# Two SBUF pools trade places and one look-up table moves behind a later product, in a three-stage kernel on one core

## The chip, the cores and the metric

The kernel runs on one core of a Trainium2 chip. The metric is device microseconds of one execution, the median of a few runs. The core has a matrix engine (PE, with its weight loads in a row of their own, PEld), a vector engine (DVE), an engine for activations and copies (ACT), GpSimd (POOL), and a queue engine (SP) that issues most DMAs. Each engine works through its own list of instructions in order, and they wait for each other by semaphores.

## The reference

Three layers, one after the other, in float32:

```python
# attention over 4 x 8 heads, 576 tokens, head size 64
proj = x @ w_phi;  proj -= max(abs(proj));  phi = [exp(proj), exp(-proj)]      # for q and for k
kv = phi(k).T @ v;  z = sum(phi(k));  x = (phi(q) @ kv) / (phi(q) @ z + 1e-6)
# experts: each of 2304 tokens goes to one of 8
logits = x @ w_gate + bias[modality];  e = argmax(logits);  g = softmax(logits)[e]
x[tokens of e] = g * (relu(x[tokens of e] @ w1[e]) @ w2[e])
# last products
out = ((x @ w_a) * (x @ w_b)) @ w_out
```

Float32 products of the last two layers are made of three matmuls each, on a high and a low part of both operands (`mm3`, L53 to L56).

## The kernel before, in words

**Attention** runs in rounds, each on one group of heads (eight groups; rounds 0 to 8, a round also finishes what the round before it began). `phi` (L125) projects raw q and k (`qk`, pool `a_ld`, two buffers of 9216 bytes a partition), subtracts the maximum and leaves the differences `df` (pool `a_df`, five buffers of 4096 bytes). `turn` transposes a `df` on PE (`qtp`) and ACT writes its exponentials (`qts`). `kx` multiplies exponentials of k with v (`kxp`, copied by DVE to `kx`), `num` makes the numerator and denominator (`nmp`), and DVE divides (`rec`, `x`, L237 to L242). Within the rounds PE's order is the order of the code; on the other engines, and everywhere after the rounds, a scheduler that simulates a timeline sets it when the program is built.

**Routing** handles the tokens in two halves; `Route.steps` (L339) lists what is done for one half: gate, rank, place, table. `table` makes two look-up tables by one-hot matmuls: `tbp` gives `idx`, the rows that the experts gather, and `tbq` gives `perm` and `g2`, the way back and the squared gate weight, which only the last stage reads. POOL builds the one-hots of the first half, DVE those of the second. The first half's table stands in round 7, before `phi(1)` (L924); the second half's steps are side work of the expert stage (L952).

**Experts** (`Moe`, L520 to L603) take four tiles of up to 608 tokens, two for each half. A tile gathers its tokens in five pieces (`xg`, L561), transposes them (`mxt`, L573) and splits them into high and low (`mxh` on ACT, `mxl` on DVE). Eight blocks of weights are loaded (`s`, two buffers) and split (`wh` on ACT, `wl` on DVE, three buffers). Eight `hp` products of 24 matmuls each follow, their results split into `hh` (ACT) and `hl` (DVE), and then `yp` products, copied out by ACT. `hp` and `yp` share three PSUM buffers. The pools of this stage lie on the same side of SBUF that `a_ld` and `a_df` held: `m_w` (the `wh` and `wl`, 24 KB) first, `m_xt` (the `mxh` and `mxl`, 19 KB) behind it. A tile of a new pool waits until the last reader of what lay there has finished.

As further side work each half of the last layer's weights is converted: a load `raw` (SP), `cvs` on ACT, `cvs` on POOL, then `cvt`, `cvt`, `cvs`, `cvs`, `wsum` on DVE (L691 to L698), sums, a split `whi` (ACT, one buffer), and a store from which the buffer comes free.

**Last products** (from some 400 us to the end) keep PE busy nearly throughout.

Of the kernel before, what the change touches and what calls it, by code (L numbers as in the profile page):

```python
# [10 lines left out]
F32 = mybir.dt.float32  # L11
F32R = mybir.dt.float32r
BF16 = mybir.dt.bfloat16
I32 = mybir.dt.int32
AF = mybir.ActivationFunctionType
ALU = mybir.AluOpType
# [4 lines left out]
P = 128  # L21
B, H, S, D = 4, 8, 576, 64
NTOK = B * S
HALF = NTOK // 2
# [4 lines left out]
NG = 9  # L29
# [3 lines left out]
NTMAX = (HALF + E * (TS - 1)) // TS  # L33
KMAX = (HALF + TS - 1) // TS
NSUB = (TS + P - 1) // P
YC = HALF + CG
TB = 6
# [21 lines left out]
class Attn:  # L59
    def __init__(self, nc, tc, ctx, cst, qk, v, vt, xs, lgp):  # L60
        self.nc, self.tc = nc, tc
        self.qk, self.v, self.vt, self.xs = qk, v, vt, xs
        self.cst, self.lgp = cst, lgp
        pool = lambda n, b, **kw: ctx.enter_context(tc.tile_pool(name=n, bufs=b, **kw))
        self.p_ld = pool("a_ld", 2, side="right")
        self.p_df = pool("a_df", 5, side="right")
        self.p_v = pool("a_v", 3)
        self.p_x = pool("a_x", 2)
        self.p_sm = pool("a_sm", 4)
        self.p_kx = pool("a_kx", 2)  # L70
        self.p_qt = pool("a_qt", 11)
        self.p_vt = pool("a_vt", 2)
        self.p_kp = pool("a_kp", 4)
        self.p_kt = pool("a_kt", 3)
        self.ps_p = pool("aps_p", 2, space=PSUM)
        self.ps_q = pool("aps_q", 2, space=PSUM)
        self.ps_c = pool("aps_c", 2, space=PSUM)
        self.u = {}
# [185 lines left out]
def consts(nc, pool, keep, w_phi, w_gate):  # L264
    c = {}
    ident = c["ident"] = keep.tile([P, P], F32, name="ident")
    w = c["wp"] = pool.tile([P, P], F32, name="wp")
    nc.scalar.dma_start(out=w[0:64, :], in_=w_phi)
    nc.scalar.dma_start(out=w[64:128, :], in_=w_phi)
    make_identity(nc, ident)  # L270
    mask = c["mask"] = pool.tile([P, 2], F32, name="mask")
    wg = c["wg"] = pool.tile([P, 4, 16], F32, name="wg")
    nc.gpsimd.memset(wg, 0.0)
    src = w_gate.rearrange("(p h d) e -> h d p e", h=2, d=64)
    for h in range(2):
        rows = slice(64 * h, 64 * h + 64)
        nc.gpsimd.memset(mask[rows, h:h + 1], 0.0)
        nc.gpsimd.memset(mask[rows, 1 - h:2 - h], -1000.0)
        nc.gpsimd.dma_start(out=wg[rows, :, 8 * h:8 * h + 8], in_=src[h])
    return c  # L280
# [53 lines left out]
class Route:  # L334
# [4 lines left out]
    def steps(self, wk, ps, tag, after=None):  # L339
        self.wk, self.ps, self.tag = wk, ps, tag  # L340

        def start():
            with self.tc.issue_after(after) if after else nullcontext():
                self.cst = route_consts(self.nc, wk)
            self.gate()

        return [start, self.rank, self.place, self.table]

    def w(self, shape, name, dt=F32):
        return self.wk.tile([P] + shape, dt, tag=name, name=name)  # L350
# [45 lines left out]
    def place(self):  # L396
# [66 lines left out]
        self.meta = self.pool.tile([1, 3 * NTMAX + 1], I32, name=f"meta{self.bp}")  # L463
        nc.vector.tensor_copy(self.meta, meta[0:1, :])

    def table(self):
        nc, c = self.nc, self.cst
        NC = NTMAX * NSUB
        gp = self.w([3, NG], "gp", BF16)
        rest = self.w([NG], "grest")  # L470
        nc.vector.tensor_copy(rest, self.gt)
        for i in range(3):
            nc.vector.tensor_copy(gp[:, i, :], rest)
            if i < 2:
                nc.vector.tensor_sub(rest, rest, gp[:, i, :])

        def onehot(out, i, v, n):
            if not self.bp:
                for g in range(NG):
                    nc.gpsimd.tensor_scalar(out=out[:, g, :], in0=c[i][:, :n], scalar1=v[:, g:g + 1], scalar2=None,  # L480
                                            op0=ALU.is_equal)
                return
            nc.vector.tensor_tensor(out=out, in0=c[i][:, :n].unsqueeze(1).to_broadcast([P, NG, n]),
                                    in1=v.unsqueeze(2).to_broadcast([P, NG, n]), op=ALU.is_equal)

        def lookup(name, col, n, row, parts):
            k = len(parts)
            hot = self.w([NG, n], name + "h", BF16)
            rhs = self.w([NG, k, n], name + "r", BF16)
            lhs = self.w([NG, P], "lhs" if self.bp else name + "l", BF16)  # L490
            onehot(hot, "icol", col, n)
            for i, v in enumerate(parts):
                (nc.vector if self.bp else nc.gpsimd).tensor_mul(rhs[:, :, i, :], hot, v.unsqueeze(2).to_broadcast([P, NG, n]))
            onehot(lhs, "i128", row, P)
            ps = self.ps.tile([P, 512], F32, tag=self.tag, name=name)
            for g in range(NG):
                nc.tensor.matmul(ps[:, :k * n], lhs[:, g, :], rhs[:, g].rearrange("p a n -> p (a n)"),
                                 start=g == 0, stop=g == NG - 1)
            return [ps[:, i * n:(i + 1) * n] for i in range(k)]

        def token(out, hi, lo, base):
            t = self.w([NC], "tk")[:, :hi.shape[1]]
            nc.vector.tensor_scalar(out=t, in0=hi, scalar1=float(1 << TB), scalar2=float(base), op0=ALU.mult, op1=ALU.add)
            nc.vector.tensor_add(out, t, lo)

        toks = [c["tokp"][:, i, :] for i in range(2)]
        self.idx = self.pool.tile([P, NC], I32, name=f"idx{self.bp}")
        self.g2 = self.pool.tile([P, NG], F32, name=f"g2{self.bp}")
        self.perm = self.pool.tile([P, NG], I32, name=f"perm{self.bp}")
        hi, lo = lookup("tbp", self.col, NC, self.pl, toks)  # L510
        token(self.idx, hi, lo, 0)
        hi, lo, *gs = lookup("tbq", self.cq, NG, self.cl, toks + [gp[:, i, :] for i in range(3)])
        token(self.perm, hi, lo, HALF * self.bp)
        nc.vector.tensor_copy(self.g2, gs[2])
        nc.vector.tensor_add(self.g2, self.g2, gs[1])
        nc.vector.tensor_add(self.g2, self.g2, gs[0])
        nc.vector.tensor_mul(self.g2, self.g2, self.g2)
# [362 lines left out]
def low(tc, step):  # L880
    def run():
        with tc.high_priority(offset=-LOWR):
            step()

    return run
# [3 lines left out]
def trn_kernel(ctx, tc, qk, v, vt, w_phi, mod_id, w_gate, bias, wm, wf, out):  # L889
    nc = tc.nc  # L890
# [9 lines left out]
    with ExitStack() as actx:  # L900
        cpool = actx.enter_context(tc.tile_pool(name="const", bufs=1))
        wkpool = actx.enter_context(tc.tile_pool(name="rwork", bufs=1))
        lgp = [(cpool, keep)[i].tile([P, NG, E], F32, name=f"lgp{i}") for i in range(2)]
        with tc.tile_pool(name="warm_ps", bufs=1, space=PSUM) as wps:
            z = cpool.tile([P, 512], BF16, name="warm")
            nc.vector.memset(z, 0.0)
            wz = wps.tile([P, 512], F32, name="warmp")
            for i in range(NWARM):
                nc.tensor.matmul(wz, z[:, :P], z, start=i == 0, stop=i == NWARM - 1)
        cst = consts(nc, cpool, keep, w_phi, w_gate)  # L910
        cst["warm"] = z
        at = Attn(nc, tc, actx, cst, qk, v, vt, xs, lgp)
        at.load(0)
        for r in range(9):
            if r + 1 < 8:
                at.load(r + 1)
            if r == 2:
                bs = bias_load(nc, cpool, keep, bias, mod_id)
                routes = [Route(tc, rpool, lgp[i], bs[i], i) for i in range(2)]
                rsteps = [low(tc, st) for st in routes[0].steps(wkpool, at.ps_c, "c", at.first)]  # L920
            if r == 0:
                order = ExitStack()
                order.enter_context(tc.manual_schedule(engines={mybir.EngineType.PE}))
            at.round(r, {4: {2: rsteps[:1]}, 5: {2: rsteps[1:3]}, 7: {0: rsteps[3:]}}.get(r, {}) if r > 2 else {})  # L924
            if r == 8:
                order.close()
    with ExitStack() as mctx:
# [21 lines left out]

        wk1 = rctx.enter_context(tc.tile_pool(name="rwork1", bufs=1, **tl))  # L950
        rs = routes[1].steps(wk1, ps_t, "t")
        side = {k: [low(tc, rs[f])] for f, k in enumerate((0, 3, 5, 8))}  # L952
        side[9] = [close_work]

        def conv(f):
# [24 lines left out]
        with tc.If(nts[0] > NTMIN, label="extra"):  # L980
            n = slice(3 * NTMAX, 3 * NTMAX + 1)
# [4 lines left out]
    side = {}  # L986
# [65 lines left out]
```

## Time and profile before

| | |
|---|---|
| runs of the kernel before | 828.99 to 831.8 us, median 831.49 us (3 runs) |
| the profiled execution | 832.01 us, its span 830.2 us, mean granted clock 0.996 |
| PE busy | 800.1 us (96%), 7283 matmuls |
| DVE busy | 597.2 us (72%) |
| ACT busy | 375.7 us (45%) |
| POOL busy | 136.3 us (16%) |

The timeline has four stretches of interest here: the last attention rounds (141 to 166 us), the first expert tile with the first conversions (166 to 220), the stretch to the third tile (220 to 260), whose tokens come from the second half, and the rest. In a row of the timeline the first number is the start, the second the length; "[1.88 <-DVE mxl L577]" says that the engine had been idle for 1.88 us and what ended that. The length of a single matmul overlaps the next one, so the step between two matmuls is the difference of their starts.

### The profile page before, as it was taken

Reading aid. Unit: us, or ns where it says so; the run is one execution under the profiler, and the core shown is the slowest. Engines: PE = TensorE matmul, PEld = TensorE weight load, DVE = VectorE, ACT = ScalarE, POOL = GpSimd, SP = SyncE. Lnnn points to the kernel's source line nnn. Section 1 sums busy time; section 2 is a strip of 40 time slices with the busy share of each in tenths; the row PEclk is TensorE's granted clock in tenths of the full one; section 3 lists DMA queues with packets and bytes.
Section 4 is the critical chain, followed back from the end, with each engine's and each line's share of the span. In section 5 each row is a group of like instructions: output and inputs, shape, how many; then the busy total and the mean of one; then the engine's idle time right before and its main releaser. Section 6 shows DMA issues by size and latency. Waiting matters only on the chain.

```text
span 830.2 us, 18334 instructions
## 1 busy us (share of the span) xinstructions
PE 800.1 (96%) x7283; PEld 752.1 (91%) x7284; DVE 597.2 (72%) x1071; ACT 375.7 (45%) x665; POOL 136.3 (16%) x164
## 2 busy tenths in 40 slices
PE   8999999999997999999899999999999999999996
PEld 7989888889997999999799899989999999999995
DVE  6877898779997999996698755675554485445553
ACT  4555555535443564554444433553333354333332
POOL 1000009442225623220121000020000002000002
PEclk9999999999999999999999999999999999999999
DMA  8756432576768887976689866576656668565632
GB/s 301 227 148 177 151 117 82 155 229 218 275 215 288 295 332 246 318 267 229 233 309 324 288 229 212 198 257 209 226 199 199 195 209 291 203 201 184 224 129 87
DMA packets 85163, 184.22 MB, mean 222 GB/s; under 512 B 27760, under 2 KB 37520, under 8 KB 85072
## 3 DMA queue, kind: packets, MB, share of 16 engines
q1 hardware_dynamic: 81872, 173.21, 61.7%
q0 software_dynamic: 3040, 9.72, 3.5%
q8 instruction: 58, 0.95, 0.5%
q14 instruction: 33, 0.27, 0.1%
q10 hardware_dynamic: 160, 0.07, 0.0%
HBM read 145.21 MB, written 37.75 MB: 220 GB/s over the span
## 4 chain that ended last, share of the span: by engine, by line
PE 30%; issue 16%; DVE 2%; ACT 1%; DMA 1%; POOL 0%; POOLq 0%; SPq 0%; DVEq 0%; ACTq 0%
PE abp L54 6%; PE abp L56 6%; PE abp L55 6%; PE op L56 4%; PE op L55 4%; PE op L54 4%; DMA wsc<-whi 1%; POOL out L797 0%; DVE ca L827 0%; ACT pc L841 0%; DVE gl L829 0%; ACT yh L744 0%; DVE d L850 0%; DVE yl L745 0%; DVE ca L855 0%
## 5 line engine op out<-in xcount | busy, mean ns | idle before, releaser
L841 ACT COPY pc<-abp 128x384 f32<-128x384 f32 x252 | 120.4, 479 | 201.7 <-PE abp L56 196.5
L54 PE MATMUL abp<-yh,fw 128*128 128x384 f32 x504 | 169.9, 337 | 2.8 <-ACT pc L841 1.8
L55 PE MATMUL abp<-yl,fw 128*128 128x384 f32 x504 | 169.9, 337 | 0.0
L56 PE MATMUL abp<-yh,fw 128*128 128x384 f32 x504 | 169.9, 337 | 0.0
L54 PEld LDWEIGHTS abp<-yh,fw 128*128 128x128 f32 x504 | 94.6, 188 | 12.1 <-ACT pc L841 3.1
L55 PEld LDWEIGHTS abp<-yl,fw 128*128 128x128 f32 x504 | 94.6, 188 | 7.5
L56 PEld LDWEIGHTS abp<-yh,fw 128*128 128x128 f32 x504 | 94.6, 188 | 0.0
L690 POOL TENSOR_SCALAR cvs<-cvs 128x768 f32<-128x768 f32 x24 | 61.7, 2573 | 196.2 <-ACT cvs L689 147.6
L56 PE MATMUL op<-fw,gl 128*128 128x512 f32 x216 | 85.2, 394 | 1.2 <-DVE gl L829 1.2
L54 PE MATMUL op<-fw,gh 128*128 128x512 f32 x216 | 85.4, 395 | 1.0 <-ACT gh L828 1.0
L55 PE MATMUL op<-fw,gh 128*128 128x512 f32 x216 | 85.4, 396 | 0.0
L54 PE MATMUL hp<-mxh,wh 128*128 128x304 f32 x256 | 78.8, 308 | 1.9 <-DVE hl L591 0.9
L56 PE MATMUL yp<-hh,wl 128*128 128x304 f32 x256 | 77.6, 305 | 1.1 <-DVE wl L553 1.1
L55 PE MATMUL hp<-mxl,wh 128*128 128x304 f32 x256 | 77.9, 305 | 0.0
L54 PE MATMUL yp<-hh,wh 128*128 128x304 f32 x256 | 76.8, 304 | 0.8 <-ACT y L603 0.7
L56 PE MATMUL hp<-mxh,wl 128*128 128x304 f32 x256 | 77.5, 303 | 0.0
L55 PE MATMUL yp<-hl,wh 128*128 128x304 f32 x256 | 77.3, 303 | 0.0
L797 POOL DMA_INDIRECT out<-o,perm x18 | 18.1, 1005 | 354.0 <-ACT o L796 347.5
L190 ACT ACTIVATE qts<-qtp 128x512 f32<-128x512 f32 (+1 forms) x80 | 38.3, 558 | 59.9 <-PE qtp L187 59.9
L850 DVE TENSOR_TENSOR d<-u,pc 128x768 f32<-128x768 f32 x36 | 34.4, 956 | 33.4 <-ACT pc L841 33.3
L552 ACT CAST wh<-s 128x1024 fp32r<-128x1024 f32 x32 | 33.6, 1050 | 42.6 <-PE hp L55 24.4
L828 ACT CAST gh<-ca 128x384 fp32r<-128x384 f32 x72 | 36.9, 515 | 32.7 <-DVE ca L827 32.7
(191 smaller groups left out, 1602.1 us busy)
## 6 DMA issues: line engine op xcount, KB each, us to landing
fw<-wsc SPq DMA_DIRECT2D x72, 512.0 KB, 4.3
fw<-wsc SPq DMA_DIRECT2D x144, 256.0 KB, 3.3
raw<-in_moe_w SPq DMA_DIRECT2D x24, 768.0 KB, 5.3
s<-in_moe_w SPq DMA_DIRECT2D x32, 512.0 KB, 4.7
fw<-wsc SPq DMA_DIRECT2D x72, 128.0 KB, 2.7
wsc<-whi SPq DMA_DIRECT2D x12, 640.0 KB, 5.4
wsc<-wsum SPq DMA_DIRECT2D x12, 640.0 KB, 5.3
wsc<-whi SPq DMA_DIRECT2D x12, 512.0 KB, 3.6
```

What stands on the lines that cost most here:

```text
L54: nc.tensor.matmul(out, lh, rh, start=start, stop=False)
L55: nc.tensor.matmul(out, lh, rl, start=False, stop=False)
L56: nc.tensor.matmul(out, ll, rh, start=False, stop=stop)
L190: nc.scalar.activation(t[:, s, :n, :], ps[:, :n, :], AF.Exp, scale=1.0 - 2.0 * s)
L552: nc.scalar.copy(hi, src)
L690: nc.gpsimd.tensor_scalar(out=s.bitcast(F32), in0=s.bitcast(F32), scalar1=LEAST, scalar2=None, op0=ALU.max)
L797: st = nc.gpsimd.indirect_dma_start(out=self.out[:, :], out_offset=bass.IndirectOffsetOnAxis(ap=self.routes[bp].perm[:, c:c + 1], axis=0), ...
L828: nc.scalar.copy(gh, ca[:, i, :])
L841: nc.scalar.copy(x, ps)
L850: nc.vector.tensor_add(d, u, x.unsqueeze(1).to_broadcast([P, 2, n]))
```

## The change

It has two parts. First, the pool `a_df` is made before `a_ld`. The differences then lie where `m_w` comes later, together with some 4 KB of a `qk` tile; the rest of the `qk` tiles lies under `m_xt`. Before, the `qk` tiles and about a tile and a half of `df` lay under `m_w`, and the rest of `df` under `m_xt`. Second, `table` is cut in two: what makes `tbq`, `perm` and `g2` becomes a fifth step, `back`, which for the first half stands in round 8 behind the last `kx`; for the second half it follows `table` in the same place.

```diff
+        self.p_df = pool("a_df", 5, side="right")
         self.p_ld = pool("a_ld", 2, side="right")
-        self.p_df = pool("a_df", 5, side="right")
...
-        return [start, self.rank, self.place, self.table]
+        return [start, self.rank, self.place, self.table, self.back]
...
     def table(self):
+        n = NTMAX * NSUB
+        self.toks = [self.cst["tokp"][:, i, :] for i in range(2)]
+        self.idx = self.pool.tile([P, n], I32, name=f"idx{self.bp}")
+        hi, lo = self.lookup("tbp", self.col, n, self.pl, self.toks)
+        self.token(self.idx, hi, lo, 0)
+
+    def back(self):
+        nc = self.nc
         gp = self.w([3, NG], "gp", BF16)
...
-        hi, lo = lookup("tbp", self.col, NC, self.pl, toks)
-        token(self.idx, hi, lo, 0)
-        hi, lo, *gs = lookup("tbq", self.cq, NG, self.cl, toks + [gp[:, i, :] for i in range(3)])
-        token(self.perm, hi, lo, HALF * self.bp)
+        hi, lo, *gs = self.lookup("tbq", self.cq, NG, self.cl, self.toks + [gp[:, i, :] for i in range(3)])
+        self.token(self.perm, hi, lo, HALF * self.bp)
...
-            at.round(r, {4: {2: rsteps[:1]}, 5: {2: rsteps[1:3]}, 7: {0: rsteps[3:]}}.get(r, {}) if r > 2 else {})
+            at.round(r, {4: {2: rsteps[:1]}, 5: {2: rsteps[1:3]}, 7: {0: rsteps[3:4]}, 8: {0: rsteps[4:]}}.get(r, {}) if r > 2 else {})
...
-        side = {k: [low(tc, rs[f])] for f, k in enumerate((0, 3, 5, 8))}
+        side = {}
+        for f, k in enumerate((0, 3, 5, 8, 8)):
+            side.setdefault(k, []).append(low(tc, rs[f]))
```

The helpers `onehot`, `lookup` and `token` become methods with the same instructions; lines behind them move down by two or three. Since the scheduler builds the whole order anew, instructions move in other places as well.

The first place is PE from the last `turn` of attention to the first `hp`. Before, it read (`kxp` is the last product of k and v, `mxt` the transposes of the first tile):

```order
L187 MATMUL qtp<-ident,df 128x128 x8
L211 MATMUL kxp<-v,kp 64x73 x8
...
L211 MATMUL kxp<-v,kt 64x73 x2
L573 MATMUL mxt<-ident,xg 128x128 x4
L231 MATMUL nmp<-kx,qts 64x73 x40
L573 MATMUL mxt<-ident,xg 128x128 x4
L573 MATMUL mxt<-ident,xg 128x96 x4
L54 MATMUL hp<-mxh,wh 128x304
```

Now it reads, on PE in the same stretch:

```order
L187 MATMUL qtp<-ident,df 128x128 x8
L575 MATMUL mxt<-ident,xg 128x128 x6
L211 MATMUL kxp<-v,kp 64x73 x8
...
L211 MATMUL kxp<-v,kt 64x73 x2
L486 LDWEIGHTS tbql
L486 MATMUL tbq<-tbqr,tbql 128x45
...
L575 MATMUL mxt<-ident,xg 128x128 x2
L575 MATMUL mxt<-ident,xg 128x96 x4
L231 MATMUL nmp<-kx,qts 64x73 x40
L54 MATMUL hp<-mxh,wh 128x304
```

The nine `tbq` matmuls, which stood some way above the first piece (between `tbp` and a `pjp` product), now stand behind `kxp`, and all transposes of the tile stand ahead of `nmp`.

The second place is DVE at the same time, as it reads now (`kx` is the copy that both parts of `nmp` read; the `g_2938` rows make `g2`):

```order
L555 TENSOR_TENSOR wl<-s,wh 128x1024 x2
L321 MEMSET ones 128x128
L579 TENSOR_TENSOR mxl<-mxt,mxh 128x4x128
L382 MEMSET oh 128x4
L217 COPY kx<-kxp 128x292
L493 TENSOR_SCALAR tk<-tbq 128x9
...
L517 TENSOR_TENSOR g_2938<-g_2938,tbq 128x9
L237 TENSOR_SCALAR rec<-nmp 128x4
L555 TENSOR_TENSOR wl<-s,wh 128x1024
L518 TENSOR_TENSOR g_2938<-g_2938,tbq 128x9
```

Two `wl` now stand ahead of the `kx` copy where one stood, and the last reader of `tbq` stands behind the third `wl`. The attention stage has two PSUM buffers for `kxp`, `tbq` and `nmp` alike; the second part of `nmp` (24 matmuls) takes the one that `tbq` held, so it waits for that last reader.

The third place is ACT behind the handoff. Before, ACT read from the last split of the first tile's tokens:

```order
L576 CAST mxh<-mxt 128x4x96
L689 ACTIVATE cvs<-raw 128x768
L372 ACTIVATE ex<-lg 128x72
L590 ACTIVATE hh<-hp 128x608
L689 ACTIVATE cvs<-raw 128x768
L552 CAST wh<-s 128x1024
```

Now it reads there:

```order
L578 CAST mxh<-mxt 128x4x96
L554 CAST wh<-s 128x1024
L691 ACTIVATE cvs<-raw 128x768
L372 ACTIVATE ex<-lg 128x72
L691 ACTIVATE cvs<-raw 128x768
L592 ACTIVATE hh<-hp 128x608
L554 CAST wh<-s 128x1024
```

The second conversion's `cvs` stands ahead of the first `hh`. Some rows below, the second `whi` (128x1280) stood behind the last two `hh` of the tile and now stands ahead of them. On DVE the second conversion's `cvt`, `cvt`, `cvs` and `wsum` of the first, with a `wl`, stand between the first and the second `hl`, where only one `cvs` of each kind and a `wl` stood. POOL's rows for `tbq` have not moved. On PE the transposes that begin the third tile stand 24 matmuls (one `hp`) earlier than before, and on DVE a `wl` and an `hl` that stood ahead of the second half's `idx` stand behind it. From the start of the last products on, every engine's order is as before.

## Rows read from the trace of the kernel before

**Rows 1.** PE's waits by what ended them, 140 to 260 us (us in total, times, longest).
```profile
PE yp L56 <- DVE wl L553: 1.1, 1, 1.1
PE hp L54 <- DVE hl L591: 0.9, 3, 0.4
```

**Rows 2.** Windows: length, busy time of PE, PEld, DVE, ACT, POOL, PEclk, DMA share, GB/s.
```profile
160.00:210.00 50.00, 46.31 (x407) 44.71 (x403) 43.81 (x91) 22.35 (x33) 14.90 (x10) 1.00 0.66 222
210.00:250.00 40.00, 38.75 (x283) 38.01 (x282) 40.00 (x92) 20.11 (x28) 11.24 (x5) 1.00 0.68 230
250.00:260.00 10.00, 5.74 (x38) 5.55 (x38) 9.38 (x14) 1.86 (x3) 8.78 (x5) 0.83 0.74 236
260.00:390.00 130.00, 130.00 (x943) 129.99 (x942) 113.88 (x151) 66.95 (x93) 37.74 (x17) 1.00 0.81 292
```

**Rows 3.** Timeline of PE: start, length, instruction, idle time before and its releaser.
```profile
143.25 0.39 PE L497 MATMUL tbq<-tbqr,tbql 128*128 128x45 bf16 x9 [0.83 <-POOL tbqr L493]
...
162.35 0.66 PE L573 MATMUL mxt<-ident,xg 128*128 128x128 f32 x4 [1.88 <-DVE mxl L577]
...
162.97 2.76 PE L231 MATMUL nmp<-kx,qts 128*64 128x73 f32 x80
...
166.43 0.38 PE L54 MATMUL hp<-mxh,wh 128*128 128x304 f32 x1
...
169.40 0.37 PE L54 MATMUL hp<-mxh,wh 128*128 128x304 f32 x1 [0.91 <-DVE x L242]
```

**Rows 4.** Timeline of DVE at the handoff and in the first conversions.
```profile
161.61 0.68 DVE L577 TENSOR_TENSOR mxl<-mxt,mxh 128x512 fp32r<-128x512 f32 x1
...
162.37 0.45 DVE L217 COPY kx<-kxp 128x292 f32<-128x292 f32 x1
...
166.21 1.22 DVE L553 TENSOR_TENSOR wl<-s,wh 128x1024 fp32r<-128x1024 f32 x1 [0.36 <-ACT wh L552]
...
175.64 0.56 DVE L691 TENSOR_SCALAR cvt<-cvs 128x768 int32<-128x768 int32 x1 [1.85 <-POOL cvs L690]
...
176.33 0.95 DVE L693 SCALAR_TENSOR_TENSOR cvt<-raw,cvt 128x768 int32<-128x768 int32 x1
...
202.49 0.78 DVE L591 SCALAR_TENSOR_TENSOR hl<-hp,hh 128x608 fp32r<-128x608 f32 x1
```

**Rows 5.** Timeline of ACT from the last differences to the first written weight.
```profile
159.37 1.07 ACT L552 CAST wh<-s 128x1024 fp32r<-128x1024 f32 x1
...
165.13 1.05 ACT L552 CAST wh<-s 128x1024 fp32r<-128x1024 f32 x1 [1.50 <-DMA s<-in_moe_w]
...
172.47 0.90 ACT L689 ACTIVATE cvs<-raw 128x768 f32<-128x768 f32 x1 [5.15 <-DMA raw<-in_moe_w]
...
173.43 0.66 ACT L590 ACTIVATE hh<-hp 128x608 fp32r<-128x608 f32 x1
...
177.37 0.91 ACT L689 ACTIVATE cvs<-raw 128x768 f32<-128x768 f32 x1 [3.29 <-DMA raw<-in_moe_w]
...
195.83 1.04 ACT L715 CAST whi<-wsum 128x1024 fp32r<-128x1024 f32 x1
...
204.76 1.26 ACT L715 CAST whi<-wsum 128x1280 fp32r<-128x1280 f32 x1 [1.27 <-DMA wsc<-whi]
```

**Rows 6.** Timeline of SP's DMA queue: start of issue, time to the next.
```profile
161.72 3.52 SPq L544 DMA_DIRECT2D s<-in_moe_w  x2
...
165.35 0.37 SPq L685 DMA_DIRECT2D raw<-in_moe_w  x1
...
167.84 1.01 SPq L685 DMA_DIRECT2D raw<-in_moe_w  x1
```

**Rows 7.** DMA issues by line: count, KB each, median us to landing.
```profile
raw<-in_moe_w SPq DMA_DIRECT2D x24, 768.0 KB, 5.3
```

**Rows 8.** Timeline of POOL: one conversion step of 768 columns.
```profile
178.36 2.14 POOL L690 TENSOR_SCALAR cvs<-cvs 128x768 f32<-128x768 f32 x1 [2.76 <-ACT cvs L689]
```

**Rows 9.** Timeline of PE: the transposes that wait for the second route's first gather.
```profile
256.30 0.94 PE L573 MATMUL mxt<-ident,xg 128*128 128x128 f32 x4 [4.26 <-DMA xg<-xs,idx]
```

More of the change, by code (lines that the diff above doesn't have):

```diff
@@ L464, in place, with onehot, lookup, token @@
         nc.vector.tensor_copy(self.meta, meta[0:1, :])
-    def table(self):
-        nc, c = self.nc, self.cst
-        NC = NTMAX * NSUB
+    def onehot(self, out, i, v, n):
+        nc, src = self.nc, self.cst[i][:, :n]
+        if not self.bp:
+            for g in range(NG):
+                nc.gpsimd.tensor_scalar(out=out[:, g, :], in0=src, scalar1=v[:, g:g + 1], scalar2=None, op0=ALU.is_equal)
+            return
+        nc.vector.tensor_tensor(out=out, in0=src.unsqueeze(1).to_broadcast([P, NG, n]),
+                                in1=v.unsqueeze(2).to_broadcast([P, NG, n]), op=ALU.is_equal)
+    def lookup(self, name, col, n, row, parts):
+        nc, k = self.nc, len(parts)
+        hot = self.w([NG, n], name + "h", BF16)
+        rhs = self.w([NG, k, n], name + "r", BF16)
+        lhs = self.w([NG, P], "lhs" if self.bp else name + "l", BF16)
+        self.onehot(hot, "icol", col, n)
+        for i, v in enumerate(parts):
+            (nc.vector if self.bp else nc.gpsimd).tensor_mul(rhs[:, :, i, :], hot, v.unsqueeze(2).to_broadcast([P, NG, n]))
+        self.onehot(lhs, "i128", row, P)
+        ps = self.ps.tile([P, 512], F32, tag=self.tag, name=name)
+        for g in range(NG):
+            nc.tensor.matmul(ps[:, :k * n], lhs[:, g, :], rhs[:, g].rearrange("p a n -> p (a n)"),
+                             start=g == 0, stop=g == NG - 1)
+        return [ps[:, i * n:(i + 1) * n] for i in range(k)]
+    def token(self, out, hi, lo, base):
+        nc = self.nc
+        t = self.w([NTMAX * NSUB], "tk")[:, :hi.shape[1]]
+        nc.vector.tensor_scalar(out=t, in0=hi, scalar1=float(1 << TB), scalar2=float(base), op0=ALU.mult, op1=ALU.add)
+        nc.vector.tensor_add(out, t, lo)
+    def table(self):
+        n = NTMAX * NSUB
[4 more added lines that the diff above has]
+    def back(self):
+        nc = self.nc
         gp = self.w([3, NG], "gp", BF16)
@@ L475, in table @@
                 nc.vector.tensor_sub(rest, rest, gp[:, i, :])
[L477 to L507, printed above, removed]
         self.g2 = self.pool.tile([P, NG], F32, name=f"g2{self.bp}")
         self.perm = self.pool.tile([P, NG], I32, name=f"perm{self.bp}")
-        hi, lo = lookup("tbp", self.col, NC, self.pl, toks)
```

## Prediction

> **What bounds the kernel now.** Read the windows first [rows 2]. PE is the engine to follow: from 260 to 390 us it has no idle time at all, and before that it has holes. From 210 to 250 DVE is busy 40.00 of 40 us, so there it is DVE that paces PE; from 160 to 210 DVE still has 6.2 us idle. Then the waits of PE [rows 1] and the timeline around its holes [rows 3, 9]: 0.83 us ahead of `tbq`, 1.88 ahead of a transposing `mxt`, 0.91 within the first `hp`, 0.9 in three waits on `hl`, 1.1 in the first `yp` and 4.26 at the third tile's tokens. The change touches the first three, 3.6 us together. Everything is summed against the profiled execution, 832.01 us, which is 0.5 above the median of 831.49; the last products keep their order, so a PE that is late at 400 us ends late by the same.
>
> **Term 1, the handoff from attention to the experts: +0.7 us.** Moving `tbq` takes its wait and its matmuls from round 7 (0.83 + 0.39 = 1.2 us [rows 3]), and as DVE's next reduction stands right behind, I carry these 1.2 us through to the last `kxp`. With the pools exchanged `mxh` and `mxl` of the first pieces come early, but `wh` now waits for the last differences to be turned, and two `wh` and two `wl` come in a row. The first `wh` starts 1.2 us earlier than at 159.37 [rows 5], so its `wl` runs from 159.25 and the second to 161.6, at 1.2 each [rows 4]; then `mxl` 0.68 and the `kx` copy 0.45 [rows 4]. The copy ends at 162.7, where it ended before (162.8). PE meanwhile waits some 1.6 us for this `mxl` ahead of its last `mxt`: the old hole of 1.88 is not removed, it changes its name. The first part of `nmp` (16 of 40 matmuls, 1.1 of 2.76 us [rows 3]) ends at 164.0. Its second part needs the PSUM buffer of `tbq`, whose last reader on DVE stands behind the third `wl`. That `wl` needs the third `wh`, which needs a load that is issued when the first `wl` has freed its buffer, at 160.5; before, the issue at 161.72 [rows 6] was followed by the `wh` at 165.13 [rows 5], 3.4 us later. So the load lands at 163.9, `wh` ends at 165.0, `wl` at 166.2, the additions at 166.4, and PE has stood 2.4 us for a wait that did not exist. The second part takes 1.66, and `hp` starts at 168.05. Before, it started at 166.43 and lost 0.91 inside [rows 3], in effect 167.35. Bounds: -1.5 (if the load is there early, this wait is gone and 2.2 of it come back) and +1.5 (the 0.91 comes again).
>
> **Term 2, the first `hp` products: +3.3.** The first two `raw` loads stand behind the second part of `nmp`: issued at 165.35 and 167.84 before [rows 6], 1.3 after the second part began; now 167.7 and 168.0. Their data were used 7.1 and 9.5 us after issue (ACT at 172.47 and 177.37 [rows 5]), against a median landing of 5.3 [rows 7]. I take the 7.1 and 9.5, since both are issued at once now, with a load of 512 KB just ahead. The first `cvs` is then at 174.8 to 175.7, POOL's step of 2.14 [rows 8] ends at 177.85, DVE's two `cvt` (0.5 and 0.9 from start to start [rows 4]) at 179.2, and the first `hl` behind them at 180.0. ACT is no later: the second `cvs` at 177.5, then `hh` (0.66 [rows 5]), 179.0. PE has three PSUM buffers for `hp`, so it wants the first back after 72 matmuls of 0.139 us, at 178.05: a wait of 1.9. The second `hl` stands behind the second conversion's `cvt`, `cvt` and a `wl` and a `wsum`: POOL ends that one at 180.55, and 0.5 + 0.9 + 0.9 + 1.2 + 0.9, with the small rows less, lets `hl` end at 185.6. PE was ready after 24 matmuls at 183.3: 2.3 more. Less the 0.9 of the three old waits [rows 1]: 4.2 - 0.9 = +3.3. With landings at the median the same chain gives +0.9, the lower bound; the upper is +4.5, loads 1.2 later. The Trainium skill ("DMA: Bandwidth & Descriptors", "Issuing engines are not separate DMA queues") says that all transfers share the same 16 DMA engines and interleave; by it two loads issued together should both land late, as the 9.5 us against 5.3 would suggest.
>
> **Term 3, the first `yp`: +2.8, less 1.1.** Before, no wait stood there until 1.1 us behind a `wl` [rows 1]. In DVE's new list there are, from the second to the sixth `hl`, five `hl` at 0.7, three rows of 1024 columns at 1.15, five conversion rows at 0.9 and four at 0.5, and four of 256 columns at 0.34 (an estimate by width): 14.5 us from 184.9, so the sixth ends at 199.4. PE asks for its PSUM buffer at 185.6 + 4 x 3.34 = 199.0: 0.4. The second `whi` now stands ahead of the last two `hh`, and has to wait for the store of the first: from the first to the second it took 8.9 us (195.83 to 204.76 [rows 5], the last 1.27 of them idle on that store). With the first at 192.8 (its sums are at that place in the same list) the second ends at 203.0, `hh` at 203.6, `hl` at 204.4, where PE wants them at 201.9: 1.7 and 0.7. The 1.1 later goes, since PE is by then later than DVE. Bounds 0 (the store lands in time) and +5 (the first `whi` stands behind a `cvs` that waits for its load, up to the 5.15 seen [rows 5]).
>
> **Term 4, the third tile: -0.7.** The last `hl` of the tile ends near 206.4 instead of 203.3 [rows 4]. From there DVE has no idle time to 250 [rows 2], so the second half's `idx` would be 3.1 late; a `wl` and an `hl` less stand ahead of it (-2.0), some small rows more (an estimate, +0.6): 1.7 late. The gathered tokens let PE go on at 258.0 instead of 256.30 [rows 9], and the 24 `hp` matmuls now behind that point are 3.34: in all 5.0 late, where terms 1 to 3 made 5.7. The gather is thus a wall: whatever is won ahead of it counts only if `idx` comes earlier too. The granted clock of 0.83 in 250 to 260 [rows 2] (3.4 us at the lower level, 1.7 lost) stays, as PE still waits some 3.6 there.
>
> **Term 5, the rest: +0.9.** From 260 to 390 DVE is busy 114 of 130 us [rows 2], so a late DVE catches up slowly; I allow one more set of `hl` waits like the old (0.9 [rows 1]), from 0 to +3.
>
> The rest is nothing: POOL's one-hots of `tbq` stay, hidden ahead of the gathers; the later `perm` and `g2` are read only in the last stage.
>
> **Sum.** 0.7 + 3.3 + 2.8 - 1.1 - 0.7 + 0.9 = +5.9: 837.9 in the profiled execution's terms, 837.4 as a median.
>
> **The rivals.** *Not slower, by the gather.* The `raw` loads land at the median, `hl` are never late, and the 3.6 us of holes go. For: 5.3 is what most loads take [rows 7]. Against: two loads at once, and `tbq`'s buffer. Then the price of the first tile is nothing, but the gather decides: 3.34 of `hp` behind it, with `idx` 1.4 earlier by its list and up to 3.6 by the earlier start, gives 3.34 - 5.0 = -1.7, or 829.8; if the stretch at the lower clock goes as well, 828. It decides as soon as the second part of `nmp` starts before 165. *No change.* Term 1 holds, term 2 is at its lower bound, term 3 at 0: 0.7 + 0.9 - 1.1 and the gather's +1.9 at most, 832 to 834. *Slower still, by the clock.* PE stands 1.6 and 2.4 us within 5 us, then 1.9 and 2.3. In the rows a hole of 1.88 kept the full clock (1.00 in 160 to 210 [rows 2]) and one of 4.26 lost it; if these bring the lower level once, 1.7 us are lost, and with term 5 at its upper end it is 837.4 + 1.7 + 2.1 = 841. The Trainium skill ("TensorE: Matmul & The Clock Gate", "HAM oscillation — how this bites in real kernels") says that short idle spells between bursts can send the array back to half rate again and again; the windows here show that only for the longest hole.
>
> **How the numbers follow.** 0.62 for the sum (own range 834 to 842), 0.13 for not slower, 0.14 for no change, 0.11 for the clock. A measurement of this kernel can tell 0.5%, 4.15 us, from no change. Slower needs above 835.65: nine tenths of the sum's chance (the rest is its lower end, with small terms 2 and 3) and all of the clock's, 0.56 + 0.11 = 0.67. Faster needs below 827.3, which the first rival reaches if `idx` gains another microsecond: about half of its chance, 0.07. The rest, 0.26, is no change. The range runs from 830.5 (most of the first rival left out) to 844.5 (terms 2, 3 and 5 near their upper ends together).
>
> **What would show it.** After the last `kxp` PE's waits should name `mxl` (about 1.6) and then a wait inside `nmp` on a DVE row of `g2` (about 2.4). The first `hp` rows should show two waits on `hl` near 2 us each, with ACT idle on `raw`, and the first `yp` waits behind `hh` and `hl` with `whi` behind its store. The third tile's `mxt` should resume one to three us later. If `nmp` runs on without a wait, term 1 is wrong; if both `raw` are used within 6 us, term 2 is; if the first `hl` comes before PE asks and the median is still above 835, the cause lies where I have not looked.

## The result, and the profile after

The changed kernel takes 837.06 us in the median of 7 runs (834.87 to 841.84), the kernel before 831.49 (827.85 to 835.13). The ratio is 1.0066, its 95% interval 1.0045 to 1.0086; a ratio here need not be the quotient of the two medians, it can be some 0.001 off. In a later repeat it was 1.0077 (1.0058 to 1.0097). The forecast was 837.4. The profiled execution took 835.86 us, its span 834.1, its mean granted clock 0.988 against 0.996.

PE's waits from 140 to 260 us, as in [rows 1] (us in total, times, longest):

```profile
PE mxt L575 <- DMA xg<-xs,idx: 6.0, 1, 6.0
PE nmp L231 <- DVE rec L238: 2.6, 1, 2.6
PE mxt L575 <- DVE oh L382: 1.9, 1, 1.9
PE hp L54 <- DVE hl L593: 1.4, 1, 1.4
PE yp L54 <- DVE hl L593: 0.7, 1, 0.7
```

The wait for `tbq` and the one on `x` are gone, the hole ahead of `mxt` is still there, and a new one stands in `nmp`. Its place in time, and what follows, on PE (start, length, instruction, idle time before it):

```profile
160.01 0.55 PE L575 MATMUL mxt<-ident,xg 96*128 96x96 f32 x4 [1.86 <-DVE oh L382]
...
164.36 3.19 PE L231 MATMUL nmp<-kx,qts 128*64 128x73 f32 x48 [2.64 <-DVE rec L238]
167.48 0.62 PE L54 MATMUL hp<-mxh,wh 128*128 128x304 f32 x1
167.90 0.46 PE L55 MATMUL hp<-mxl,wh 128*128 128x304 f32 x1
168.15 0.46 PE L56 MATMUL hp<-mxh,wl 128*128 128x304 f32 x1
...
172.06 0.30 PE L54 MATMUL hp<-mxh,wh 128*128 128x304 f32 x1
172.20 0.30 PE L55 MATMUL hp<-mxl,wh 128*128 128x304 f32 x1
...
254.37 1.09 PE L575 MATMUL mxt<-ident,xg 128*128 128x128 f32 x4 [5.99 <-DMA xg<-xs,idx]
```

The second part of `nmp` (48 rows) took 3.19 us, where all 80 took 2.76 before [rows 3], and from 167.90 six `hp` matmuls stand 0.25 or a little less apart, before the step is 0.14 again: about half the rate. The granted clock from 160 to 170 us tells the same (first row the kernel before, second the changed one; the number before the last two):

```profile
160.00:170.00 10.00, 7.22 (x125) 6.60 (x121) 8.88 (x24) 4.96 (x8) 3.94 (x5) 1.00 0.60 200
```

```profile
160.00:170.00 10.00, 7.35 (x97) 6.97 (x98) 5.62 (x25) 1.52 (x2) 1.70 (x4) 0.66 0.84 272
```

DVE at that place:

```profile
159.88 0.45 DVE L217 COPY kx<-kxp 128x292 f32<-128x292 f32 x1
...
162.92 1.23 DVE L555 TENSOR_TENSOR wl<-s,wh 128x1024 fp32r<-128x1024 f32 x1 [0.54 <-ACT wh L554]
164.06 0.16 DVE L518 TENSOR_TENSOR g<-g,tbq 128x9 f32<-128x9 f32 x1
```

PE goes on 0.14 us after the last reader of `tbq` has ended; the profile names a neighbouring row, `rec`, as the releaser. In the same way it names `oh` ahead of `mxt`, where an `mxl` had ended 0.06 us before. The windows of [rows 2] for the changed kernel (length, busy PE, PEld, DVE, ACT, POOL, PEclk, DMA share, GB/s):

```profile
160.00:210.00 50.00, 45.22 (x371) 44.04 (x372) 44.07 (x98) 19.51 (x27) 13.71 (x9) 0.93 0.69 230
210.00:250.00 40.00, 38.38 (x291) 38.03 (x289) 39.23 (x86) 20.93 (x29) 14.51 (x6) 1.00 0.62 209
250.00:260.00 10.00, 5.63 (x30) 5.66 (x31) 6.25 (x10) 0.89 (x2) 8.78 (x5) 0.66 0.94 317
260.00:390.00 130.00, 128.61 (x930) 128.28 (x929) 114.28 (x152) 66.15 (x91) 35.57 (x16) 1.00 0.81 289
```

One thing must be taken off before the two profiles are compared. Well ahead of the place that the change touches, the same projection of attention and the look-up `tbp` behind it (first the kernel before, second the changed one) stand at

```profile
123.09 1.16 PE L154 MATMUL pjp<-wp,qk 64*128 64x128 f32 x16 [0.93 <-DVE vals L414]
...
141.88 0.55 PE L497 MATMUL tbp<-tbpr,tbpl 128*128 128x90 bf16 x9
```

```profile
121.07 1.16 PE L154 MATMUL pjp<-wp,qk 64*128 64x128 f32 x16 [0.93 <-DVE vals L414]
...
139.52 0.55 PE L486 MATMUL tbp<-tbpr,tbpl 128*128 128x90 bf16 x9
```

The projection stands 2.0 us earlier in the changed kernel and `tbp` 2.4, from short idle times that change from run to run: in the repeat of the changed kernel the same projection stands at 122.60. So 2.36 us are added below to the changed kernel's times wherever the two profiles are compared; this is called the frame of `tbp`. In it PE goes on at the gather at 256.73, 0.4 later than before [rows 9], with 3.3 us of `hp` more to do.

### The profile page after: what moved, and what is told of

The parts are those of the page before. It is cut to its first block, busy times and chain, and to the rows that moved or that the text cites. A ratio compares the mean times of both kernels' runs of the same rounds, so it can differ in the third digit from the quotient of the medians.

```text
span 834.1 us, 18338 instructions
## 1 busy us (share of the span) xinstructions
PE 802.4 (96%) x7283; PEld 754.8 (90%) x7284; DVE 597.7 (72%) x1071; ACT 376.4 (45%) x665; POOL 138.3 (17%) x164
## 4 chain that ended last, share of the span: by engine, by line
PE 30%; issue 16%; DMA 2%; DVE 2%; ACT 1%; SPq 1%; POOL 0%; POOLq 0%; DVEq 0%; ACTq 0%
PE abp L54 6%; PE abp L55 6%; PE abp L56 6%; PE op L56 4%; PE op L55 4%; PE op L54 4%; DMA raw<-in_moe_w 1%; DMA wsc<-whi 1%; SPq L729 1%; POOL out L799 0%; ACT pc L843 0%; DVE ca L829 0%; DVE gl L831 0%; ACT yh L746 0%; DVE yl L747 0%
## 5 line engine op out<-in xcount | busy, mean ns | idle before, releaser
L156 DVE TENSOR_REDUCE m<-pjp 128x8 f32<-128x1024 f32 (+2 forms) x49 | 45.1, 933 | 10.4 <-PE pjp L154 10.4
L54 PEld LDWEIGHTS hp<-mxh,wh 128*128 128x128 f32 x256 | 49.0, 192 | 3.5 <-issue 3.1
```

The lines of the kernel that those rows point to most:

```text
L54: nc.tensor.matmul(out, lh, rh, start=start, stop=False)
L156: nc.vector.tensor_reduce(out=mv, in_=pv, op=ALU.max, axis=AX.X, apply_absolute_value=True)
```

## The experiments

Theory G: the gathered tokens of the third tile arrive when `idx` and DVE let them, whatever PE did before; each `hp` that the new order puts behind that point is added to the time. Theory H: the loss is made at the handoff, by the wait for `tbq`'s buffer and what follows it. The runs stood on three chips: the kernel before took 831.77 us beside the first four, 838.24 beside the next four and 831.53 beside the last four. So ratios are compared, each with the kernel before on the same chip, and microseconds are worked out from them.

**One part of the change at a time.** The first run has only the first hunk of the change's diff (the pools), the second all but this hunk.

> The pools exchanged, tbq left in round 7. In this kernel's order the transposes that begin the third tile stand 48 hp matmuls ahead of the last hp, as in the changed kernel (24 in the kernel before). Theory G (what counts is the gather of the third tile: matmuls that stand behind its wait can't cover it): about as slow as the changed kernel, 3 to 5 us over the kernel before (834.5 to 836.5), with a wait of 5 to 7 us on the gathered tokens. Theory H (what counts is the handoff: the wait of nmp for the last reader of tbq, and the lower clock behind it): the wait of 2.6 us in nmp is gone and the clock stays at 1.00 in 160 to 170, so 4 to 5 us faster than the changed kernel, at or under the kernel before (828 to 832).

> The second table moved behind the last k-v product, the pools left as they were. Here too the third tile's first transposes stand 48 matmuls ahead of the last hp. Theory G: 3 to 5 us slower than the kernel before (834.5 to 836.5), with a wait of 5 to 7 us at the gather. Theory H: between the two parts of nmp stand 8 transposes here, which cover part of the wait for the last reader of tbq; about 1 us over the kernel before (832 to 833).

Measured: 836.08 us, ratio 1.0039 (1.0017 to 1.0062), and 842.03 us, ratio 1.0118 (1.0083 to 1.0153). Either part alone is slower than the kernel before, and the table alone is slower than both together (their intervals just touch). The first falls where G put the time, without any wait in `nmp` and with the clock at 1.00 from 160 to 170; H is refuted for it. G's wait of 5 to 7 us did not come, though: PE waits 3.28 us at the third tile there, and another 3.0 had been lost at the first `yp`:

```profile
PE mxt L573 <- DVE wsum L716: 3.3, 1, 3.3
PE yp L55 <- DVE hl L591: 3.0, 1, 3.0
PE mxt L573 <- DVE oh L382: 2.1, 1, 2.1
PE hp L54 <- DVE hl L591: 1.8, 1, 1.8
```

The second lost more than either theory gave; its PE waits twice for `mxl`, in `nmp`, for `hl` and at the gather:

```profile
PE mxt L575 <- DMA xg<-xs,idx: 6.1, 1, 6.1
PE mxt L575 <- DVE mxl L579: 2.7, 2, 1.5
PE hp L54 <- DVE hl L593: 2.5, 2, 1.4
PE nmp L231 <- DVE g L518: 2.1, 1, 2.1
PE yp L54 <- DVE hl L593: 0.6, 1, 0.6
```

**The third tile's transposes held back on PE.** Nothing else is edited; `issue_after` lets them stand on PE only behind the last matmul of the second tile's last `hp`. (`mm3` returns its last matmul for this.) The scheduler leaves the handoff's order as it was.

```diff
-                mm3(nc, ps[:, g, :CG], wh[:, i, :], wl[:, i, :], T["xh"][:, c, gs], T["xl"][:, c, gs], c == 0, c == 3)
+                last = mm3(nc, ps[:, g, :CG], wh[:, i, :], wl[:, i, :], T["xh"][:, c, gs], T["xl"][:, c, gs], c == 0, c == 3)
+        T["hp", f] = last.ins
...
                 for i in order.get(j, ()):
-                    self.transp(Ts[n + 1], i)
+                    with self.tc.issue_after(T["hp", 7]) if n == 1 and NT > 1 else nullcontext():
+                        self.transp(Ts[n + 1], i)
```

On the changed kernel:

> The changed kernel with one edge more: the third tile's transposes may stand on PE only behind the last hp matmul of the second tile (48 matmuls, 6.7 us later). The handoff is untouched. Theory G: the wait of 6.0 us at the gather goes, and with it the stretch at the lower clock behind it (1.7 us): 829 to 831.5, under the changed kernel by 6 to 8 us. Theory H: the 5.6 us of the handoff stay and only what the changed kernel lost at the gather beyond the kernel before comes back (1.7 us): 834 to 836.

On the kernel before:

> The kernel before with the same edge: its third tile's transposes move back by 24 hp matmuls (3.3 us). Theory G: of the 4.3 us wait 3.3 go, and the clock stays at the higher level (1.7 us): 825.5 to 828. Theory H says nothing against a gain here, but if the wait at the gather is only where an earlier lateness of DVE shows, the wait moves to an hl or a yp behind it and the time stays at 830 to 832.

Measured: 830.78 us, ratio 0.9994 (0.9969 to 1.0018), and 829.01 us, ratio 0.9957 (0.9937 to 0.9977). On the changed kernel the edge alone takes back all of the loss, with the handoff's wait as long as ever and the lower clock behind it:

```profile
PE hp L54 <- DVE hl L594: 2.6, 3, 1.4
PE nmp L231 <- DVE rec L238: 2.6, 1, 2.6
PE yp L54 <- DVE hl L594: 2.0, 1, 2.0
PE mxt L575 <- DVE oh L382: 1.9, 1, 1.9
```

No row for the gathered tokens is left. The kernel before gains too, but less, 3.6 us: its wait at the gather was shorter [rows 9], with 24 `hp` matmuls behind it instead of 48. Its 829.01 us miss the 825.5 to 828 that G gave. So with the transposes held the change still costs 0.9994 - 0.9957 = 0.0037, or 3.1 us, by the two intervals give or take some 2.6. What is left in this way is the handoff and the new lists of DVE and ACT together, and G is not the whole of it.

**The suspected cost doubled without the change.** In the kernel before, the last two `hp` are put behind the third tile's first transposes, where one stood:

```diff
-                self.l1(T, 2 * j)
-                self.l1(T, 2 * j + 1)
+                with self.tc.issue_after(Ts[n + 1]["tr", 0]) if early and j == 3 else nullcontext():
+                    self.l1(T, 2 * j)
+                    self.l1(T, 2 * j + 1)
```

(`early` is the second tile; its `transp(Ts[n + 1], 0)` is called ahead of this.)

> The kernel before, with neither part of the change, but the last two hp products of the second tile (48 matmuls) are put behind the third tile's first transposes on PE; in the kernel before it was one product (24). Pools, tables and handoff are as before. Theory G (the gather's arrival sets when PE goes on, and each hp behind that point is added): 24 x 0.139 = 3.3 us more, 834 to 836.5, so that more than half of what the whole change cost is had without either part of it; the wait at the gather grows to 7 to 8 us. Theory H (the loss is made at the handoff and in DVE's list): nothing at the handoff moves, so 830 to 832.5.

Measured: 842.08 us against 838.24 on that chip, ratio 1.0059 (1.0037 to 1.0082), 4.9 us (3.8 by the medians; G gave 3.3). On G's side: most of the loss of the whole change, with neither part of it. The estimate in absolute time missed, since the kernel before is 6.5 us slower on that chip. Three of its waits, the first as long as G gave it:

```profile
PE mxt L573 <- DMA xg<-xs,idx: 7.1, 1, 7.1
PE mxt L573 <- DVE mxl L578: 1.9, 1, 1.9
PE tbq L497 <- DVE tbqr L493: 1.5, 1, 1.5
```

**The handoff's wait taken away.** In `back` of the first half, `tbq` gets a buffer of the other PSUM pool (`ps2` is attention's `ps_q`):

```diff
+        if not self.bp:
+            self.ps, self.tag = self.ps2, "q"
         hi, lo, *gs = self.lookup("tbq", self.cq, NG, self.cl, self.toks + [gp[:, i, :] for i in range(3)])
```

> The changed kernel, with tbq in a buffer of the other PSUM pool (that of qtp), so that the second part of nmp does not wait for the last reader of tbq. In its order the third tile's transposes stand behind the last hp, as in the third run. Theory G together with H: the wait of 2.6 us in nmp and the lower clock behind it (some 2 us) go, and the gather is no wall: 825 to 828, 3 to 5 us under the third run (830.8). If G alone held and the handoff cost nothing (what is won there is given back behind), 829.5 to 832.

Measured: ratio 0.9972 (0.9953 to 0.9991), 835.18 against 838.24. The wait in `nmp` is gone; against the third run (0.9994) this is 1.8 us, in the right direction, less than the 3 to 5 expected and with intervals that overlap. The order behind the handoff was built anew here, so the 1.8 is not the price of that wait alone. And a lower clock was there without the wait: behind a hole of 1.85 us the 80 rows of `nmp` took 4.36 us (2.76 before [rows 3]), with a granted clock of 0.70 from 170 to 175.

**The handoff's hole filled.** On the third run's kernel:

```diff
+        if u == 7 and len(parts) == 2:
+            z, fp = self.cst["warm"], self.ps_q.tile([P, 4, P], F32, tag="q", name="filp")
+            for i in range(10):
+                nc.tensor.matmul(fp.rearrange("p g f -> p (g f)"), z[:, :P], z, start=i == 0, stop=i == 9)
         ps = self.ps_c.tile([P, 6, 73], F32, tag="c", name="nmp")
```

> The third run's kernel with ten matmuls of 512 columns (some 2.2 us, into a PSUM buffer that nobody reads) between the two parts of nmp, where PE waits 2.6 us. They take nothing from the wait itself. If the hole is what brings the lower clock, PE's granted clock stays at 1.00 in 160 to 170, the second part of nmp takes 1.7 us instead of 3.2 and the first hp matmuls run at full rate: 1.5 to 2.5 us under the third run, 828 to 829.5. If the clock falls for another reason, or what is won there is lost again to the hl behind, 830 to 832.

Measured: ratio 0.9984 (0.9965 to 1.0003), 0.8 us under the third run, within what the runs can't tell apart. PE:

```profile
168.34 2.21 PE L235 MATMUL nmp<-kx,qts 128*64 128x73 f32 x32
170.89 2.48 PE L225 MATMUL filp<-warm 128*128 128x512 bf16 x9 [0.34 <-issue]
173.31 1.75 PE L235 MATMUL nmp<-kx,qts 128*64 128x73 f32 x48
```

Behind the fill the second part took 1.75 us, not 3.19, as expected; but the first part, ahead of the fill, was already at about half rate (2.21 us for 32 rows, 1.23 in the third run), so the clock did not stay up as expected. It was back at the higher level behind the fill; what the hole of 2.6 us alone does to it is not shown.

**Further back.** On the sixth kernel and on the kernel before, the transposes are held behind the first `yp` product instead (`T["yp", 0]`, taken in `l2` as `T["hp", f]` in `l1`).

> The sixth kernel (tbq in the other PSUM pool) with the third tile's transposes held on PE behind the first yp product of the second tile (48 yp matmuls, 6.7 us further). If a wait for the gathered tokens is still left in the sixth run, it goes here: 824 to 827. If none is left there, the two are equal within 1 us.

> The kernel before with the third tile's transposes held behind the first yp product of the second tile (24 hp and 48 yp matmuls later than in the kernel before; in the fourth run 24 hp). If the 0.5 us that were left at the gather in the fourth run were all, it is equal to the fourth run (ratio 0.994 to 0.997). If the tokens are often later than in that one profile, it is 1 to 2 us better; if the late transposes delay mxh and mxl of the third tile until its first hp asks for them, it is 1 us or more worse.

Measured: ratios 1.0009 (0.9987 to 1.0030) and 1.0048 (1.0030 to 1.0065), 3 us over the sixth run and 7.6 over the fourth. The first is a miss. The second is worse, which its last case allowed, but not for the reason given there: the third tile's first `hp` waits only 0.43 us for `mxh`. No wait for tokens is left in either, but others came: in the first 2.77 us for a `y` copy at 288 us, with the clock at 0.93 and 0.89 in the ten microseconds before 290 and after it; in the second 3.41 us for an `hl` at 367, with 0.80 and 0.86 before and after 370:

```profile
367.44 0.59 PE L54 MATMUL hp<-mxh,wh 128*128 128x304 f32 x1 [3.41 <-DVE hl L591]
```

What in their order makes these waits was not followed up.

**The parts with the gather out of the way, and the changed kernel again.**

> The first run's kernel (pools exchanged, tbq in round 7) with the third tile's transposes held on PE behind the second tile's last hp (48 matmuls). Theory G: with the gather out of the way the exchange of pools costs little by itself, 829 to 832 against a kernel before of 831.5, 4 to 6 us under the first run. If the exchange has a cost of its own (first conversions and yp waits at 182 and 206 us, 4.8 us in the first run's trace), the wait only moves and the ratio stays over 1.002.

> The second run's kernel (table moved, pools as before) with the same edge. Theory G: its 6.1 us at the gather go, with the lower clock behind it: 833 to 836 against 831.5, so 6 to 8 us come off the second run's 842, and what is left (2 to 4 us) is the handoff, where nmp waits 2.15 us for the last reader of tbq and mxt twice for mxl. If G explained all of it, 830 to 832.

> The changed kernel, unchanged, on the same chip as the three others. Its ratio to the kernel before was 1.0066 (1.0045 to 1.0086); a ratio within that interval is expected, and a trace with waits of 2.6 us in nmp and 5.5 to 6.5 us at the gather. If the stretch of lower clock between 160 and 170 us is a matter of chance, it may be missing here.

Measured: 1.0014 (0.9998 to 1.0030), 1.0031 (1.0015 to 1.0048) and 1.0077 (1.0058 to 1.0097). The first two come out within half a microsecond of what G gave: the pools alone cost next to nothing once the gather is out of the way. The third has the ratio and the wait in `nmp` (2.50) that were expected, and again the lower clock from 160 to 170 (0.69), but its wait at the third tile is 4.14 us, not 5.5 to 6.5:

```profile
256.28 1.09 PE L575 MATMUL mxt<-ident,xg 128*128 128x128 f32 x4 [4.14 <-DVE hl L593]
```

This pair of profiles of one kernel shows the wall itself. In the frame of `tbp` PE came to the gather at 250.74 us in the first profile and at 252.90 in the repeat's, 2.2 later, and went on at 256.73 and 257.04, 0.3 later: what had been lost ahead was taken from the wait. All ratios of this design, with the gain from the edge in us of 831.5:

| | as built | transposes held | gain |
|---|---|---|---|
| before | 1 | 0.9957 | 3.6 |
| pools only | 1.0039 | 1.0014 | 2.1 |
| table only | 1.0118 | 1.0031 | 7.2 |
| both | 1.0066, 1.0077 | 0.9994 | 6.0, 6.9 |

The gains go with the wait at the third tile (4.26, 3.28, 6.11 and 5.99 or 4.14 us in the profiles), not with the 24 or 48 matmuls that the edge moved. The lowest ratio is that of the kernel before with the edge: it beats both kernels, and can't be told from the sixth run's 0.9972.

## Why the prediction was right

**The outcome.** 837.4 was forecast, 837.06 measured, for the likeliest case. The reason held in its shape: holes that change their name, a new wait in `nmp`, and a gather that works as a wall. Of the loss of about 6 us (the mean of 1.0066 and 1.0077), some 3.1 are left when the transposes are held; the rest, roughly half, is the gather, where the changed order has 24 `hp` matmuls more behind the wait. That the sum came within 0.4 us is luck: term 1 came out above its bounds and term 2 below its own, term 3 was too large by 2.1, the last products cost 1.6 that no term has, and these errors cancel.

**Term 1 (+0.7).** The step that failed is the clock, which this term put at nothing. Both waits stood where they were expected, 1.86 for 1.6 and 2.64 for 2.4. The size was too small, because the rival of the clock came on top: `nmp`'s second part 1.5 us longer than 1.66, and six `hp` matmuls at 0.25 (0.7). In the frame of `tbp`, `hp` starts at 167.48 + 2.36 = 169.8, not 168.05: 2.5 over the old 167.35, and with the 0.7 the term is about +3.2, above its upper bound of +2.2. The rival had been put at 1.7 for one such stretch; here it is 2.2.

**Term 2 (+3.3).** Too large, and under its lower bound of +0.9: one wait of 1.45 came where two of 1.9 and 2.3 were forecast, against 0.9 in all before, so +0.5. The step that failed is the use of the loads at 7.1 and 9.5 us. They were issued together, at 166.6 and 167.0, but used after 5.9 and 7.7 us:

```profile
172.46 0.90 ACT L691 ACTIVATE cvs<-raw 128x768 f32<-128x768 f32 x1 [9.58 <-DMA raw<-in_moe_w]
...
174.69 0.91 ACT L691 ACTIVATE cvs<-raw 128x768 f32<-128x768 f32 x1 [1.18 <-DMA raw<-in_moe_w]
```

**Term 3 (+2.8 - 1.1).** Too large: 0.67 came and the 1.1 went, -0.4. (The rows that this term lists for DVE add up to 14.8 us, not 14.5; by that its first wait would have been 0.7.) The second `whi` did not wait for the store of the first; it followed 4.0 us behind it (8.9 before [rows 5]), held up by DVE's sum:

```profile
191.80 1.06 ACT L717 CAST whi<-wsum 128x1024 fp32r<-128x1024 f32 x1 [0.49 <-DVE wsum L711]
...
195.78 1.27 ACT L717 CAST whi<-wsum 128x1280 fp32r<-128x1280 f32 x1 [1.40 <-DVE wsum L718]
```

In the repeat of the changed kernel PE's wait at the first `yp` was 2.03 us instead of 0.67, so it differs from run to run.

**Term 4 (-0.7), the wall.** By their waits terms 1 to 3 come to 3.3 instead of 5.7. PE reached the gather at 250.74 in the frame of `tbp`, 1.3 earlier than before with 3.3 of `hp` left, so 2.0 late; the 1.3 between the two counts stay without an owner. It hardly mattered: PE waited 5.99 us instead of the 3.6 forecast and went on 0.4 us later than before, not 1.7, with the `hp` behind. Terms 1 to 4 were to be +5.0; in this profile they are +3.8. The reason given for the 1.7, a late `idx`, is wrong. The rows (DVE's `idx` and POOL's issue of the gather, first the kernel before, second the changed one):

```profile
248.65 0.19 DVE L504 TENSOR_TENSOR idx<-tk,tbp 128x45 int32<-128x45 f32 x1
249.58 2.67 POOL L561 DMA_INDIRECT xg<-xs,idx  x1 [5.00 <-DMA s<-in_moe_w]
```

```profile
244.93 0.18 DVE L494 TENSOR_TENSOR idx<-tk,tbp 128x45 int32<-128x45 f32 x1
245.86 3.38 POOL L563 DMA_INDIRECT xg<-xs,idx  x1 [2.96 <-DVE cvt L693]
```

In the frame of `tbp` `idx` is ready at 247.5, 1.4 us earlier than before, but from there until PE goes on it takes 9.3 us instead of 7.5. The DMA engines are busier in the last 5.3 us of that (0.97 against 0.79): a load of `s` is issued 1.4 us behind the gather, where before one was issued 3.7 us ahead of it. No run tests whether that is the cause. So the wall stood where it did for another reason than the one forecast. That the `hp` behind the gather are added to the time was argued in the prediction; the doubled run shows it (3.8 to 4.9 us for 3.3 us of matmuls). The held runs show that what can be won back is about the wait: the pools alone gave 2.1 us for 48 matmuls, 6.7 us long.

**Term 5 (+0.9).** One wait of 1.39 on an `hl` at 362 us, less the 0.73 that went at 396: +0.66. Not foreseen: from 406.70 to 476.46 the profile has 69.8 us where the kernel before has 68.1, with the clock at 0.91 and 0.92 from 410 to 430. The order there is the same as before. Five of the fourteen profiles have such a dip and take 69.7 to 70.1 us there: both of the changed kernel, and those of the fifth, sixth and tenth run. The other nine take 68.1 to 68.6, among them the kernel before and the third run. So these 1.6 us may belong to the changed kernel and be part of what the edge takes back, or be chance; that stays open.

## What to carry to other kernels

Where an engine waits for a transfer, look at what stands behind that wait in its list before looking at the waits ahead of it. Time won or lost ahead of such a wall shows in the length of the wait, and work that a rebuilt order moves behind it is added. A small edit under a scheduler moves instructions far away; here an order edge of one line 90 us behind the edit was worth as much as the edit cost. Pushing the same edge further made it worse, so it has to be measured.

## What the runs showed of the hardware that was not expected

The lower clock level at the handoff: all five profiles in which `nmp` waits 2.0 to 2.6 us right behind a hole of 1.1 to 1.9 have it between 160 and 170 us (granted clock 0.66, 0.83, 0.69, 0.86, 0.69), and the five without that wait, with a hole of 1.9 to 2.1 (in three of them another of 0.9 to 1.1 some 7 us later), do not (1.00). The mean granted clock over the whole execution was 0.982 to 0.990 in all 13 runs of the changed kernel and 0.990 to 0.996 in the 25 of the kernel before beside the repeat, so the changed kernel has more of the lower clock in nearly every run, though this does not say where. On the chip of the fifth to eighth run two profiles (the sixth and seventh) had it behind a single hole of 1.85 and 1.83, and two (the eighth, of nearly the sixth's order, and the fifth) behind 1.86 and 1.88 did not. So the length of a single hole does not decide.

On that chip the kernel before, the only one that was timed on all three, took some 6.5 us longer. Nearly all of it lies in one place: from `tbp` to the hole ahead of the first tile's `mxt` the sixth to eighth run take 26.9 us, where the changed kernel takes 20.5, and the fifth 26.3, where the kernel before does. The four profiles show PE idle there in short pieces with no releaser ("issue") from 145 us on, most of them in an `nmp` of attention, 2 to 3 us in all, and a granted clock of 0.91 from 140 to 160. None of the ten other profiles has either there (clock 1.00). What these pieces are stays open:

```profile
147.02 0.36 PE L231 MATMUL nmp<-kx,qts 128*64 128x73 f32 x4 [0.38 <-issue]
147.77 0.38 PE L231 MATMUL nmp<-kx,qts 128*64 128x73 f32 x5 [0.40 <-issue]
```
